# Deeper buffers for 64-bit weight units, uncopied probabilities for the second batch, and loads moved to mid-head

## The chip, the cores and the metric

One NeuronCore of a Trainium2 chip runs the whole kernel as one launch. The metric is the device time of a run in microseconds. TensorE is also called PE (its weight loads PEld), VectorE DVE, ScalarE ACT, GpSimd POOL, and SyncE SP.

## What is computed

The input is q, k and v of 4 batches, 12 heads, 448 positions and 64 features, in float32, and the weights of two feed-forward blocks, in 64-bit floats. The reference, cut to what matters:

```python
def _attn_ref(q, k, v, g_q, g_k):
    q_n, k_n = rmsnorm(q, g_q), rmsnorm(k, g_k)
    scores = (1.0 / np.sqrt(64)) * np.matmul(q_n, k_n.transpose(0, 1, 3, 2))
    scores = scores - np.max(scores, axis=-1, keepdims=True)
    attn = np.exp(scores)
    attn = attn / (np.sum(attn, axis=-1, keepdims=True) + 1e-09)
    return np.matmul(attn, v).astype(np.float32)

def _moe_ref(x, w_in, w_out):            # 768 -> 2048 -> 768
    r = np.maximum(x @ w_in, 0.0)
    return (r * r @ w_out).astype(np.float32)

def _moe2_ref(x, w1, w2, w3, w_out):     # 768 -> 1024 -> 1024 -> 768
    h = (x @ w1) * (x @ w2) @ w3
    return (h @ w_out).astype(np.float32)
```

The attention output is laid out as 1792 rows of 768, goes through the first block, and then through the second.

## The kernel before

**The heads.** The 48 heads (H = 12 of each batch) run through one loop, `for h in range(NH + 1)` (line 676). Iteration h makes the scores of head h in two halves of two blocks of 112 rows each (`stage_qk`, lines 513 to 527), their exponentials (`stage_exp`, lines 529 to 560), and for the head before the transposes of the probabilities (`stage_t`, lines 562 to 580), their low halves (`stage_lo`) and the product with v (`stage_v`, lines 614 to 630). At its end `head_prep(h + 2)` scales queries and keys of a later head (lines 474 to 499); line 496 is the last reader of a head's transposed queries. Between these steps `fill(n)` puts matmuls of other work into TensorE's order.

**The filler.** In iterations 0 to 12 it is `gen_w3o` (lines 272 to 293), which multiplies the weights w3 and w_out of the second block together. In iterations 13 to 24 it is `gen_moe(0)`, the two blocks on the first batch's rows, and so on, one batch behind the heads; the last batch's blocks come behind the loop. Every float32 product is three matmuls of fp32r halves (`mm3`, lines 260 to 264: high with high, high with low, low with high).

**The weight units.** Weights come as units of 384 or 512 columns. Those of `gen_w3o` (32 units) and of batch 0 (88 units) are 64-bit in HBM. A unit is loaded into a `raw64` tile by SP (line 180), its two words are worked on by ACT (line 194) and by POOL or ACT (lines 198 and 200), joined to a float32 by DVE (line 207), stored to HBM for the later batches (line 215), and split into a high half by ACT (line 226) and a low half by POOL or DVE (line 233, by the helper line 114). Later batches load the stored float32 units (line 183). `advance(u)` (lines 240 to 254) sets the order by hand: when the low half of unit i is made, loads go up to i + LOAD64_AHEAD, words to i + 3, joins to i + 2 and high halves to i + 1. There are four `raw64` buffers, each freed by the join.

**The probabilities.** The exponentials are written as float32 to a tile of the pool `p` (3 buffers). For heads from 12 on, a DMA on SP's queue copies that tile within SBUF into a tile of type fp32r, `pw` (3 buffers, line 549), and the transposes of line 570 read the copy as fp32r. Heads 0 to 11 are transposed from `p` as float32.

**Loads of a head.** Queries come transposed by `load_head(h + 3)` (line 414, two buffers `qt`), values by `load_v(h + 1)` (line 422, two buffers `v`), and every fourth iteration a group of four heads' rows by `load_group` (lines 405 and 406). All three stand at the start of the iteration, lines 678 to 681. SP issues these DMAs, the unit loads and stores and the copies in one order, and waits in that order for the buffers.

The framework orders the instructions of each engine from the program's text and its own costs, so that single instructions may stand some steps from their place in the text.

Of the kernel before, what the change touches and what calls it, by code (L numbers as in the profile page):

```python
# [8 lines left out]
F32 = mybir.dt.float32  # L9
F32R = mybir.dt.float32r  # L10
U16 = mybir.dt.uint16
U32 = mybir.dt.uint32
# [17 lines left out]
def attention_moe_kernel(  # L30
# [16 lines left out]
    B, P, H, C, D = q_nat.shape  # L47
    S = P * C
# [26 lines left out]
    JOIN_AHEAD = 2  # L75
    WORD_AHEAD = 3
    LOAD32_AHEAD = 3
    LOAD64_AHEAD = 5

    const = ctx.enter_context(tc.tile_pool(name="const", bufs=1))  # L80
    xp = ctx.enter_context(tc.tile_pool(name="x", bufs=8))
# [7 lines left out]
    t3 = ctx.enter_context(tc.tile_pool(name="t3", bufs=3))  # L89
# [9 lines left out]
    ident = const.tile([P, P], F32, name="ident")  # L99
    ident_r = const.tile([P, P], F32R, name="ident_r")  # L100
# [3 lines left out]
    def copy_on(eng, out, in_):  # L104
        if eng == "a":
            nc.scalar.activation(out=out, in_=in_, func=AF.Copy)  # L106
        elif eng == "g":
            nc.gpsimd.tensor_scalar(out=out, in0=in_, scalar1=1.0, scalar2=1.0, op0=ALU.mult, op1=ALU.mult)
        else:
            nc.vector.tensor_copy(out=out, in_=in_)  # L110
# [60 lines left out]
    def is64(i):  # L171
        return units[i][0].dtype != F32

    def load_next():
        i = pos["load"]
        src = units[i][0]
        n = src.shape[-1]
        if is64(i):
            t = t3.tile([128, 512, 2], U32, name="raw64", tag="raw64", bufs=4)
            nc.sync.dma_start(out=t[:, :n, :], in_=src.bitcast(U32).rearrange("p (n t) -> p n t", t=2))  # L180
        else:
            t = rawp.tile([128, 512], F32, name="raw", tag="raw")
            nc.sync.dma_start(out=t[:, :n], in_=src)
        raws[i] = t
        pos["load"] += 1
# [54 lines left out]
    def advance(u):  # L240
        while pos["lo"] <= min(u + SPLIT_AHEAD, NU - 1):
            i = pos["lo"]
            for k in range(pos["load"], min(i + LOAD64_AHEAD, NU - 1) + 1):
                if is64(k):
# [145 lines left out]
    def load_group(g):  # L390
        if not (0 <= g < NH // GH):
            return
        b, h0 = divmod(g * GH, H)
        qn = t1.tile([P, GH, C, D], F32, name="qn", tag="qn")
        kn = t2.tile([P, GH, C, D], F32, name="kn", tag="kn")
        if g == 0:
            nc.sync.dma_start(out=kn[:, 0:1], in_=k_nat[0, :, 0:1])
            load_head(0)
            nc.sync.dma_start(out=qn[:, 0:1], in_=q_nat[0, :, 0:1])
            load_to(0)  # L400
            nc.sync.dma_start(out=kn[:, 1:], in_=k_nat[0, :, 1:GH])
            nc.sync.dma_start(out=qn[:, 1:], in_=q_nat[0, :, 1:GH])
            load_to(1)
        else:
            nc.sync.dma_start(out=kn, in_=k_nat[b, :, h0:h0 + GH])
            nc.sync.dma_start(out=qn, in_=q_nat[b, :, h0:h0 + GH])
        grp[g] = [qn, kn, None, None]

    def load_head(h):
        if not (0 <= h < NH):  # L410
            return
        b, hh = divmod(h, H)
        t = t2.tile([128, S], F32, name="qt", tag="qt")
        nc.sync.dma_start(out=t, in_=q_t[b, hh])
        qts[h] = t

    def load_v(h):
        if not (0 <= h < NH):
            return
        b, hh = divmod(h, H)  # L420
        t = t2.tile([128, C, D], F32, name="v", tag="v")
        nc.sync.dma_start(out=t, in_=v_in[b, hh])
        vs[h] = t
# [77 lines left out]
    def stage_k(h):  # L501
        if not (0 <= h < NH):
            return
        d = heads[h]
        khl = d.pop("khl")
        ps = ps_kv.tile([128, 512], F32R, name="kv", tag="kv")
        for c in range(C):
            nc.tensor.transpose(ps[:, c * P:(c + 1) * P], khl[:, c, :], ident_r)  # L508
        kt = t2.tile([128, S], F32R, name="kt", tag="kt")
        copy_on("a", kt, ps[:, :S].bitcast(F32))  # L510
        d["kt"] = kt
# [17 lines left out]
    def stage_exp(h, s):  # L529
        if not (0 <= h < NH):  # L530
            return
        d = heads[h]
        nb, o = d.pop("nb"), d.pop("sc")
        i = h % 2
        if s == 0 and i == 0:
            sums2[h // 2] = small.tile([P, 2, C], F32, name="sm", tag="sm")
        sm = sums2[h // 2]
        c0 = 2 * s
        pp = t3.tile([P, 2, S], F32, name="p", tag="p")
        for j in range(2):  # L540
            c = c0 + j
            p = d["p"][c] = pp[:, j, :]
            nc.scalar.activation(  # L543
                out=p, in_=o[j], func=AF.Exp, scale=d["rq"][:, c:c + 1], bias=nb[:, j:j + 1],
                accum_out=sm[:, i, c:c + 1],
            )
        if h >= H:
            words = t3.tile([P, 2, S], F32R, name="pw", tag="pw")
            nc.sync.dma_start(out=words.bitcast(F32), in_=pp)
            d["p"][c0:c0 + 2] = [words[:, 0, :], words[:, 1, :]]  # L550
        if s == 1 and i == 1:
            nc.vector.tensor_scalar(out=sm, in0=sm, scalar1=1e-9, scalar2=None, op0=ALU.add)
            rs = small.tile([P, 2, C], F32, name="rs", tag="rs")
            nc.vector.reciprocal(out=rs, in_=sm)
            wide = t1.tile([P, C, 2, D], F32, name="rsw", tag="rsw")
            nc.gpsimd.tensor_scalar(
                out=wide, in0=rs.rearrange("p i c -> p c i").unsqueeze(3).to_broadcast([P, C, 2, D]),
                scalar1=1.0, scalar2=1.0, op0=ALU.mult, op1=ALU.mult,
            )
            sums2[h // 2] = wide.rearrange("p c i d -> p c (i d)")  # L560

    def stage_t(h, kc):
        if not (0 <= h < NH):
            return
        d = heads[h]
        k0, kn = KCS[kc]
        ps = ps_pt.tile([128, 512], F32, name="pt", tag="pt")
        to, one = (ps.bitcast(F32R), ident_r) if h >= H else (ps, ident)
        for c in range(C):
            nc.tensor.transpose(to[:kn, c * P:(c + 1) * P], d["p"][c][:, k0:k0 + kn], one)  # L570
        if kn == 128:
            t = t3.tile([128, 2, S], F32R, name="ptr", tag="ptr", bufs=3)
            hi, lo = t[:, 0, :], t[:, 1, :]
            d["pt"][kc] = [hi, lo]
        else:
            t = t1.tile([128, S], F32R, name="pte", tag="pte")
            hi, lo = t[:kn, :], t[kn:, :]
            d["pt"][kc] = [t]
        copy_on("a", hi, ps[:kn, :S])
        d["lo"].append((lo, ps[:kn, :S], hi.bitcast(F32)))  # L580

    def stage_lo(h):
        if not (0 <= h < NH):
            return
        d = heads[h]
        for lo, p, hi in d["lo"]:
            sub_on("v", lo, p, hi)
        d["lo"] = []
# [43 lines left out]
    def stage_x(h):  # L632
        if 0 <= h < NH and h % 2:
            x = xf[0]
            b, hh = divmod(h, H)
            nc.vector.tensor_tensor(out=x, in0=norms_to_rows(h), in1=x, op=ALU.mult)
            t = xp.tile([128, 2, S], F32R, name="x", tag="x")
            copy_on("a", t[:, 0, :], x)
            sub_on("g", t[:, 1, :], x, t[:, 0, :].bitcast(F32))
            xs[b, hh // 2] = t  # L640
# [7 lines left out]
    def fill(n):  # L648
        state["credit"] += n
        while state["gen"] is not None and state["credit"] > 0:  # L650
            try:
                k = next(state["gen"])
                state["credit"] -= k
                state["left"] -= k
            except StopIteration:
                state["gen"] = None
# [18 lines left out]
    first.close()  # L675
    for h in range(NH + 1):
        n = W3O / ((H + 1) * 6) if h <= H else MOE / (H * 6)
        load_head(h + 3)
        load_v(h + 1)
        if h % GH == 0:  # L680
            load_group(h // GH + 1)
        stage_qk(h, 0)
        fill(n)
        stage_exp(h, 0)
        if h % H != 1:
            stage_x(h - 2)
        stage_t(h - 1, 0)
        stage_t(h - 1, 1)
        fill(n)
        stage_lo(h - 1)  # L690
        if h < NH:
            v_prep(h)
        fill(n)
        stage_k(h + 1)
        stage_t(h - 1, 2)
        stage_t(h - 1, 3)
        fill(n)
        stage_lo(h - 1)
        stage_qk(h, 1)
        fill(n)  # L700
        stage_exp(h, 1)
        fill(n)
        stage_v(h - 1)
        if h % GH == 1:
            group_prep(h // GH + 1)
        head_prep(h + 2)
        if h and h % H == 0:
            fill(1e9)
            stage_x(h - 1)
            start_fill(gen_moe(h // H - 1), MOE)  # L710
# [57 lines left out]
```

## Time and profile before

| | |
|---|---|
| time of three runs | 1237.89, 1239.81, 1242.05 us (median 1239.81) |
| profiled execution | 1239.56 us, its span 1237.8 us |
| PE, PEld busy | 1166.3 us (94%), 1054.4 us (85%) |
| DVE, ACT, POOL busy | 710.7 us (57%), 727.7 us (59%), 784.9 us (63%) |
| mean granted TensorE clock | 0.986 |
| DMA | 207.63 MB, mean 168 GB/s |

The span is the time from the first to the last instruction. A matmul's end is modelled and matmuls overlap, so that PE can be busy all the time and yet not at its best pace; the granted clock is the share of the higher of TensorE's two levels, 1.2 and 2.4 GHz. A row of waits says which engine and line stood idle, for what, how long in all, how many times, and the longest. Waits of SP are those of its instruction order. A row of the timeline gives start, length, engine, line, operation, output<-input, the shape, the number of instructions merged, and in brackets the idle time before the first with what ended it.

### The profile page before, as it was taken

The numbers are of one execution on the slowest core, as the hardware profiler recorded it, in microseconds if no ns is written. First come the engines' busy times: TensorE is split into PE (matmuls) and PEld (weight loads), VectorE is DVE, ScalarE is ACT, GpSimd is POOL, SyncE is SP. The second block draws the span as 40 slices with busy tenths as digits, with TensorE's granted clock in tenths as the row PEclk, the third lists the DMA queues.
The fourth block names the chain that finished last, engine by engine and source line by source line (L and its number), as shares of the span: only waits on it lengthen the run. The fifth ranks groups of instructions, "written<-read, shape, count | busy, mean of one in ns | idle before, by whom it ended". The sixth has DMA issues, their size and how long they took to land.

```text
span 1237.8 us, 18914 instructions
## 1 busy us (share of the span) xinstructions
PE 1166.3 (94%) x6192; PEld 1054.4 (85%) x6192; DVE 710.7 (57%) x1314; ACT 727.7 (59%) x1553; POOL 784.9 (63%) x772
## 2 busy tenths in 40 slices
PE   3799999898898999999999999999999999999998
PEld 1588887787787888998998998999999999999998
DVE  6699888878888685546567555655664421012110
ACT  5888867667746655655645655656545554443342
POOL 5875434565776756765776664756766556678673
PEclk9899999999999999999999999999999999999999
DMA  6774547787888866455445455454444443433342
GB/s 214 242 227 131 159 140 218 254 272 249 280 259 257 257 192 194 132 155 147 148 127 154 140 155 161 143 154 121 141 138 120 135 136 112 113 109 105 105 120 93
DMA packets 111347, 207.63 MB, mean 168 GB/s; under 512 B 12208, under 2 KB 66704, under 8 KB 111248
## 3 DMA queue, kind: packets, MB, share of 16 engines
q1 hardware_dynamic: 107792, 200.92, 53.8%
q10 hardware_dynamic: 3456, 5.51, 1.2%
q8 instruction: 49, 0.80, 0.3%
q14 instruction: 50, 0.41, 0.1%
HBM read 149.95 MB, written 27.53 MB: 143 GB/s over the span
## 4 chain that ended last, share of the span: by engine, by line
PE 59%; DMA 4%; DVE 4%; ACT 2%; POOL 1%; issue 1%; ACTq 0%; SPq 0%; POOLq 0%; DVEq 0%
PE mm L262 17%; PE mm L264 17%; PE mm L263 17%; PE kv L622 3%; PE pt L570 2%; DMA pw<-p 2%; PE sc L525 1%; PE sc L524 1%; DMA raw<-w 1%; POOL hl L114 1%; ACT p L543 1%; DMA kn<-k_nat 1%; PE kv L508 1%; DVE nb L526 1%; DVE raw L207 0%
## 5 line engine op out<-in xcount | busy, mean ns | idle before, releaser
L114 POOL TENSOR_TENSOR hl<-raw,hl 128x384 fp32r<-128x384 f32 (+1 forms) x383 | 447.0, 1171 | 254.5 <-ACT hl L106 250.9
L106 ACT ACTIVATE hl<-raw 128x384 fp32r<-128x384 f32 (+1 forms) x416 | 233.8, 564 | 146.8 <-PE mm L264 82.0
L262 PE MATMUL mm<-x,hl 128*128 128x448 f32 (+1 forms) x832 | 311.3, 374 | 4.4 <-ACT x L106 1.8
L263 PE MATMUL mm<-x,hl 128*128 128x448 f32 (+1 forms) x832 | 307.2, 369 | 8.1 <-POOL x L114 8.1
L264 PE MATMUL mm<-x,hl 128*128 128x448 f32 (+1 forms) x832 | 306.4, 368 | 3.7 <-DVE hl L114 3.3
L262 PE MATMUL mm<-act,hl 128*128 128x448 f32 (+1 forms) x640 | 238.3, 372 | 0.0
L263 PE MATMUL mm<-act,hl 128*128 128x448 f32 (+1 forms) x640 | 235.7, 368 | 2.3 <-POOL act L114 2.3
L264 PE MATMUL mm<-act,hl 128*128 128x448 f32 (+1 forms) x640 | 235.0, 367 | 0.6 <-POOL hl L114 0.6
L543 ACT ACTIVATE p<-sc,nb,rr 112x448 f32<-112x448 f32 x192 | 137.4, 720 | 82.4 <-DVE nb L527 82.0
L263 PEld LDWEIGHTS mm<-x,hl 128*128 128x128 f32 x832 | 158.5, 190 | 21.9 <-POOL x L114 9.7
L262 PEld LDWEIGHTS mm<-x,hl 128*128 128x128 f32 x832 | 158.4, 190 | 19.6 <-ACT x L106 3.5
L264 PEld LDWEIGHTS mm<-x,hl 128*128 128x128 f32 x832 | 158.6, 191 | 18.3 <-DVE hl L114 4.0
L526 DVE TENSOR_REDUCE nb<-sc 112x1 f32<-112x448 f32 x192 | 113.2, 616 | 34.5 <-PE sc L525 33.0
L263 PEld LDWEIGHTS mm<-act,hl 128*128 128x128 f32 x640 | 122.0, 191 | 12.8 <-POOL act L114 3.6
L200 POOL TENSOR_SCALAR raw<-raw 128x384 uint32<-128x384 uint16 (+1 forms) x110 | 86.3, 785 | 73.3 <-DMA raw<-w_in 25.8
L264 PEld LDWEIGHTS mm<-act,hl 128*128 128x128 f32 x640 | 121.9, 190 | 10.9 <-POOL hl L114 1.3
L262 PEld LDWEIGHTS mm<-act,hl 128*128 128x128 f32 x640 | 122.2, 191 | 9.7 <-ACT act L106 0.2
L114 DVE TENSOR_TENSOR ptr<-pt,ptr 128x448 fp32r<-128x448 f32 x144 | 87.0, 619 | 71.7 <-ACT ptr L106 71.3
L207 DVE SCALAR_TENSOR_TENSOR raw<-raw 128x384 uint32<-128x384 uint32 (+1 forms) x120 | 86.8, 727 | 40.3 <-POOL hl L114 27.2
L114 POOL TENSOR_TENSOR act<-gf,act 128x448 fp32r<-128x448 f32 x80 | 97.8, 1223 | 9.5 <-ACT act L106 5.0
L194 ACT ACTIVATE raw<-raw 128x384 f32<-128x384 f32 (+1 forms) x120 | 70.7, 596 | 52.2 <-DMA raw<-w 19.6
L334 DVE TENSOR_TENSOR gf<-mm,r 128x448 f32<-128x448 f32 x64 | 39.8, 622 | 97.7 <-ACT r L330 97.3
(82 smaller groups left out, 1588.6 us busy)
## 6 DMA issues: line engine op xcount, KB each, us to landing
pw<-p SPq DMA_DIRECT2D x72, 392.0 KB, 4.2
raw<-f_in SPq DMA_DIRECT2D x96, 192.0 KB, 2.4
raw<-f_out SPq DMA_DIRECT2D x72, 256.0 KB, 2.7
raw<-f SPq DMA_DIRECT2D x96, 192.0 KB, 2.4
raw<-w_in SPq DMA_DIRECT2D x32, 384.0 KB, 4.4
raw<-w_out SPq DMA_DIRECT2D x24, 512.0 KB, 6.2
raw<-w SPq DMA_DIRECT2D x32, 384.0 KB, 4.9
raw<-w3o SPq DMA_DIRECT2D x48, 256.0 KB, 2.8
```

The lines of the kernel that those rows point to most:

```text
L106: nc.scalar.activation(out=out, in_=in_, func=AF.Copy)
L114: e.tensor_tensor(out=out, in0=in0, in1=in1, op=ALU.subtract)
L194: nc.scalar.activation(out=hi, in_=hi, func=AF.Prelu, scale=2.0**-112, alpha=-(2.0**32))
L200: nc.gpsimd.tensor_scalar(out=t[:, :n, 0], in0=low, scalar1=2.0**-13, scalar2=2.0**-14 - 0.5, op0=ALU.mult, op1=ALU.add)
L207: nc.vector.scalar_tensor_tensor(out=f[:, :n].bitcast(U32), in0=t[:, :n, 1], scalar=3, in1=t[:, :n, 0], op0=ALU.logical_shift_left, op1=AL ...
L262: nc.tensor.matmul(ps, w[:, 0, wk, :], x[0], start=(i == 0), stop=False)
L263: nc.tensor.matmul(ps, w[:, 0, wk, :], x[1], start=False, stop=False)
L264: nc.tensor.matmul(ps, w[:, 1, wk, :], x[0], start=False, stop=(i == last))
L334: nc.vector.tensor_tensor(out=gf, in0=ps, in1=r, op=ALU.mult)
L526: nc.vector.tensor_reduce(out=nb[:, j:j + 1], in_=o[j], axis=AX.X, op=ALU.max, negate=True)
L543: nc.scalar.activation(out=p, in_=o[j], func=AF.Exp, scale=d["rq"][:, c:c + 1], bias=nb[:, j:j + 1], accum_out=sm[:, i, c:c + 1],)
L622: nc.tensor.matmul(ps[:, :S], w, m, start=(n == 0), stop=(n == len(ops) - 1))
```

## The change

The 64-bit units get six buffers instead of four, and their loads go seven units ahead of the low half instead of five. The copy of the probabilities begins with head 24 instead of head 12; heads 12 to 23 are transposed from the float32 tile, as heads 0 to 11 are. The copies and the exponentials share one pool of five buffers. `load_head(h + 3)` and `load_v(h + 1)` move from the start of the iteration to behind the third `fill`, ahead of `stage_k`; `load_group` stays.

```diff
-    LOAD64_AHEAD = 5
+    LOAD64_AHEAD = 7
...
-            t = t3.tile([128, 512, 2], U32, name="raw64", tag="raw64", bufs=4)
+            t = t3.tile([128, 512, 2], U32, name="raw64", tag="raw64", bufs=6)
...
-        pp = t3.tile([P, 2, S], F32, name="p", tag="p")
+        pp = t3.tile([P, 2, S], F32, name="p", tag="p", bufs=5)
...
-        if h >= H:
-            words = t3.tile([P, 2, S], F32R, name="pw", tag="pw")
+        if h >= 2 * H:
+            words = t3.tile([P, 2, S], F32R, name="pw", tag="p", bufs=5)
             nc.sync.dma_start(out=words.bitcast(F32), in_=pp)
...
-        to, one = (ps.bitcast(F32R), ident_r) if h >= H else (ps, ident)
+        to, one = (ps.bitcast(F32R), ident_r) if h >= 2 * H else (ps, ident)
...
     for h in range(NH + 1):
         n = W3O / ((H + 1) * 6) if h <= H else MOE / (H * 6)
-        load_head(h + 3)
-        load_v(h + 1)
         if h % GH == 0:
             load_group(h // GH + 1)
...
             v_prep(h)
         fill(n)
+        load_head(h + 3)
+        load_v(h + 1)
         stage_k(h + 1)
```

## Rows read from the trace of the kernel before

**Rows 1.** Stages from:to, length, busy us by engine, granted clock, DMA share, GB/s

```profile
34.00:79.00 45.00, 35.07 (x159) 29.26 (x159) 35.05 (x60) 34.80 (x75) 35.25 (x34) 0.85 0.80 243
...
191.00:498.00 307.00, 279.95 (x1454) 249.34 (x1455) 237.37 (x419) 194.81 (x421) 191.56 (x198) 0.97 0.77 243
498.00:766.00 268.00, 265.64 (x1449) 242.33 (x1448) 158.80 (x285) 155.65 (x339) 177.27 (x166) 1.00 0.51 148
```

**Rows 2.** Waits of PE between 191 and 498 us

```profile
PE pt L570 <- DMA pw<-p: 11.1, 7, 2.6
PE sc L524 <- ACT p L543: 6.6, 6, 2.1
PE mm L264 <- DVE hl L114: 3.3, 2, 1.8
```

**Rows 3.** Waits of PE from 498 us to the end

```profile
PE pt L570 <- DMA pw<-p: 2.4, 3, 1.0
```

**Rows 4.** Timeline of PE, the waits ahead of two falls of the clock

```profile
320.28 0.70 PE L570 MATMUL pt<-ident_r,pw 112*128 112x112 f32 x6 [2.10 <-DMA pw<-p]
...
364.56 0.46 PE L524 MATMUL sc<-kt,qh 128*112 128x448 f32 x1 [2.13 <-ACT p L543]
```

**Rows 5.** Stretches of 5 us at those two falls, columns as in rows 1

```profile
320.00:325.00 5.00, 4.72 (x19) 4.29 (x20) 4.37 (x9) 3.47 (x8) 2.33 (x3) 0.66 0.93 316
365.00:370.00 5.00, 4.55 (x16) 3.87 (x15) 3.86 (x12) 2.46 (x6) 2.49 (x4) 0.66 0.72 194
```

**Rows 6.** The tile `pw` between 191 and 498 us, its issues and landings

```profile
L549 SPq DMA_DIRECT2D pw<-p x25: 517/517/521, 191.7 to 491.0; - x25
...
DMA to landing us min/median/max: 3.2/4.4/6.8
```

**Rows 7.** Waits of SP's queue between 191 and 498 us

```profile
SPq L180 <- DVE raw L207: 61.6, 35, 4.3
SPq L549 <- ACT ptr L106: 27.8, 8, 6.7
SPq L414 <- DVE ql L496: 25.2, 10, 7.3
```

**Rows 8.** Timeline of SP's queue, 228 to 239 us

```profile
228.51 0.67 SPq L215 DMA_DIRECT2D f_out<-raw  x1
236.59 0.33 SPq L414 DMA_DIRECT2D qt<-q_t  x1
...
238.26 0.60 SPq L180 DMA_DIRECT2D raw<-w_out  x1
```

**Rows 9.** Timeline of ACT at 244 us

```profile
244.18 0.69 ACT L194 ACTIVATE raw<-raw 128x512 f32<-128x512 f32 x1 [4.31 <-DMA raw<-w_out]
```

**Rows 10.** Groups by line, 191 to 498 us: busy us, mean ns, idle before

```profile
L194 ACT ACTIVATE raw<-raw 128x384 f32<-128x384 f32 (+1 forms) x78 | 45.7, 595 | 50.0 <-DMA raw<-w 19.6 <-DMA raw<-w_out 14.0 <-DMA raw<-w_in 11.4
```

**Rows 11.** Timeline of PE, eight fp32 transposes of an early head and the next

```profile
133.98 0.93 PE L570 MATMUL pt<-ident,p 112*128 112x112 f32 x8
134.68 0.42 PE L262 MATMUL mm<-x,hl 128*128 128x384 f32 x1
```

**Rows 12.** Timeline of PE, eight fp32r transposes of a later head and the next

```profile
251.15 0.73 PE L570 MATMUL pt<-ident_r,pw 112*128 112x112 f32 x8
251.72 0.44 PE L262 MATMUL mm<-act,hl 128*128 128x448 f32 x1
```

**Rows 13.** Timeline of SP's queue at the start

```profile
12.62 0.33 SPq L406 DMA_DIRECT2D qn<-q_nat  x1
15.75 0.35 SPq L414 DMA_DIRECT2D qt<-q_t  x1
16.15 1.37 SPq L180 DMA_DIRECT2D raw<-wo  x3
```

**Rows 14.** Waits of PE between 12 and 79 us

```profile
PE mm L263 <- POOL x L114: 6.7, 4, 2.9
```

## The prediction

> **What bounds the kernel now.** I read four views, from coarse to fine.
>
> First the busy time by stage [rows 1], cut at the places where the iterations over the heads change their filler. From 498 us on TensorE is all but full: 265.6 of 268 us at a granted clock of 1.00, for the twelve iterations 25 to 36. The twelve iterations 13 to 24 do the same matrix work (1454 matmuls against 1449) in 307 us, so this stage, and no later one, has time to give: some 39 us. Here the 64-bit weights of the first batch are converted; DVE is busy 237 us of it against 159, the DMA engines 0.77 against 0.51, and the clock is 0.97. The start is the second place: between 34 and 79 us PE is busy 35 of 45 us at a clock of 0.85.
>
> Second, what TensorE waits for in that stage [rows 2]. The largest row is the copied probabilities: the transposes wait 11.1 us in 7 waits for the copy `pw<-p` to land. Next are score matmuls waiting for the exponentials that free their PSUM (6.6) and weights whose low half is late (3.3). After 498 us the copies cost 2.4 us in 3 waits, and no other wait is listed [rows 3].
>
> Third, what those short waits do to the clock. The transposes at 320.28 us wait 2.10 us for the copy [rows 4], and the 5 us from 320 run at a granted 0.66, that is, mostly at 1.2 GHz [rows 5]. There are six such falls in the stage, all of about 0.66 over 5 us. Five come right behind a wait for `pw<-p`; the sixth, at 365 us, behind a wait of 2.13 us for an exponential [rows 4, 5]. Each loses 0.34 x 5 = 1.7 us.
>
> Fourth, why copies and loads are late: SP issues nearly all DMAs in one order, and waits in it. The stage has 25 copies, which take 3.2 to 6.8 us to land [rows 6]. SP's longest waits here are for buffers of 64-bit units (61.6), for an ACT instruction ahead of a copy (27.8, one row of several) and for the buffer of transposed queries (25.2 in 10 waits, one of 7.3) [rows 7]. One case can be followed to its end: SP is done with a store at 229.18 us, waits for the query buffer until 236.59, and the load of a `w_out` unit behind it leaves at 238.26 [rows 8]. ACT, which converts that data next, stands idle for 4.31 us until 244.18 [rows 9]. In all, ACT's first pass over the 64-bit units waits about 45 us for loads in this stage [rows 10].
>
> **The change part by part.** The sum is made against the profiled execution: 1239.56 us, its span of 1237.8 and 1.76 around it. It lies 0.25 us below the median of the runs shown (1239.81).
>
> *Probabilities of heads 12 to 23 are transposed uncopied.* Twenty-four copies go, and all stand in this stage. The waits for them go whole: the longest is 2.6 us [rows 2], less than the shortest landing time of 3.2 [rows 6], so the exponentials themselves were done before PE came. Term: -11.1 us. With them go five falls of the clock: 5 x 1.7 = -8.5 us (ends: 0 if other gaps take their place, -10.2 if all six go).
>
> The price is fp32 instead of fp32r in 192 transposes. Eight fp32 transposes of heads 0 to 11 hold PE for 0.70 us from the first start to the next instruction's [rows 11]; eight of the fp32r form for 0.57 [rows 12]. That makes 24 x 0.13 = +3.1 us (ends: 0, and +8 if they are split into short runs between other matmuls). All of it lies on PE, the bounding engine. Here a rule speaks against the change. The Trainium skill, FP8 and Floating Point Precision, section TensorE Precision Notes, says that true fp32 takes four passes through the array; by it the term would be some +41 us as an estimate. The rows show a ratio of 1.2 for transposes, so I keep 3.1.
>
> *Six buffers and seven units ahead, for the 64-bit units.* A load waits for the same join as before, but its data is used two units later. At 88 units in about 300 us that is 2 x 3.4 us more cover for a landing of a few us, so most of the 45 us in [rows 10] should go. *Loads of queries and values in mid-head* take the 7 us stalls such as that in [rows 8] off the loads behind them: the buffer is freed at the end of the iteration before, and at the new place that is half a head (some 12 us) past. The load's own user comes more than a head later, so it stays hidden. *The removed copies* also leave SP's order, with their waits for ACT. These three act on the same thing, late unit data, and go together. What of it reaches PE now is the waits for exponentials and for halves, 6.6 + 3.3, and a few smaller rows. I take -8 us (ends: 0, -12).
>
> *What is late next.* PE would now come 27.6 us earlier over the stage (11.1 + 8.5 + 8), and the same work of DVE would have to fit: 237 of some 290 us, 82%, where now it is 77% [rows 1]. ACT and DVE run in order, so some waits come back. I give back three tenths, +8 us (ends: 0, and all 27.6).
>
> *Buffers of probabilities:* heads 0 to 23 get five in place of three, which can only loosen; no listed wait was for them, so nothing. Heads 24 to 47 share five in place of three and three: taken at nothing, see the rivals.
>
> *The start.* The first weight units leave SP at 16.15 us, behind a query load that waited until 15.75; SP was free at 12.95 [rows 13]. They now leave some 3 us earlier, with two more in flight. PE waits 6.7 us there for a low half of `wo` units [rows 14], and the clock loses 0.15 x 45 = 6.8 us [rows 1]. I take -4 us (ends: 0, -10).
>
> Sum: -11.1 - 8.5 + 3.1 - 8 + 8 - 4 = -20.5, so 1239.56 - 20.5 = 1219.1, forecast **1219 us**. Stages past 498 us stay as they are.
>
> **The rivals.**
> *The stage becomes full:* the waits go and nothing comes back. 307 falls to the 268 of the next twelve iterations plus 3, and the start gives 5: 1239.6 - 36 - 5 = 1199. For it: the later stage shows that this is possible. Against: DVE would be at 88%. Chance 0.12.
> *The chain of DVE and ACT takes over:* PE's waits move from copies to exponentials and halves, and two thirds of the gain is given back: about 1232. For it: DVE's share, and in the stage POOL, ACT and DVE all wait for each other. Chance 0.14.
> *It doesn't do what it says:* loads are sooner issued but the DMA engines are the limit in this stretch, at 0.93 of their time in 320 to 325 us [rows 5], and the clock falls as before. About 1239. Against: the copies are bytes that go, and the mean is 0.77. Chance 0.08.
> *Slower, by the shared buffers:* in heads 24 to 47 an exponential may write only where words of three half-heads ago have been transposed. If that wait were felt by PE in each of the 24 heads with 1.0 us, the longest that is there now [rows 3], and brought a fall of 1.7 us in one of five, it would cost 24 x 1.34 = 32 us: 1251. It decides from 0.85 us a head, which cancels the gain. Against: those transposes stand ahead, in PE's order, of the scores that the exponential reads. Chance 0.09.
> *Four passes:* if fp32 transposes came to four times 0.57 us a run, the term would be 24 x 1.71 = 41 instead of 3: 1257. Heads 0 to 11 speak against it [rows 11]. Chance 0.02.
>
> **How the numbers follow.** My forecast has 0.55. Faster by over 0.3% (3.7 us, about what a measurement of this kernel can tell from no change) are the forecast, the full stage and the chain: 0.81. Within it is the fourth case, 0.08; slower are the two last, 0.11. The range of 1202 to 1240 takes in the chain and the case of no effect, and the lower ends of the start and of the late loads. It leaves out the slower cases and the deepest part of the full stage.
>
> **What would show it.** Right: iteration 25 starts some 16 to 20 us sooner, no wait of a transpose for `pw<-p` before it, one or two falls of the clock there in place of six, ACT's waits for 64-bit loads down to less than half, no SP wait of 7 us for the query buffer, fp32 transposes in runs of some 0.70 us, and the stages behind it as long as now. Wrong: as many falls of the clock behind other waits; DVE over 85% busy with PE waiting for exponentials; or waits of the exponentials after 498 us for the shared buffers.

## The result and the profile after

The changed kernel is slower: 1254.09 us against 1240.93 for the kernel before (medians of four runs each on one chip), a ratio of 1.0108 [1.0084, 1.0131]. One of the four runs of the changed kernel, 1607.88 us at a mean granted clock of 0.663 throughout, is in the median and not in the ratio; the other three take 1251.65 to 1255.34 us. The forecast was 1219, with a range of 1202 to 1240. The profile read below is that of the first experiment, the same kernel run again: span 1253.4 us, mean granted clock 0.989.

The stages of the changed kernel, cut where the filler changes as in [rows 1]; columns as there, the last two lines being single falls of the clock:

```profile
34.00:79.00 45.00, 38.63 (x177) 32.40 (x178) 34.73 (x63) 37.16 (x79) 33.99 (x32) 0.96 0.74 242
193.00:514.00 321.00, 286.00 (x1450) 250.14 (x1451) 233.64 (x416) 193.61 (x419) 186.45 (x196) 0.96 0.67 200
514.00:782.50 268.50, 266.29 (x1458) 243.27 (x1456) 160.34 (x286) 156.06 (x340) 177.33 (x166) 1.00 0.51 149
265.00:270.00 5.00, 2.20 (x5) 1.45 (x6) 1.88 (x4) 4.58 (x10) 1.81 (x2) 0.56 0.73 238
374.00:379.00 5.00, 4.20 (x13) 3.22 (x14) 4.39 (x12) 3.60 (x9) 3.19 (x4) 0.66 0.72 196
```

Nearly all of the loss, 14 of the 15.6 us between the two profiled spans, is in iterations 13 to 24: 321 us for 1450 matmuls, where 307 stood in [rows 1]; the twelve behind take 268.5 against 268. The bytes of the copies did go (DMA share 0.67 against 0.77), DVE is not busier, and the clock of the stage is still 0.96, with six falls as before (at 225, 265, 320, 375, 390 and 430 us). What TensorE waits for in this stage of the changed kernel (total, times, longest):

```profile
PE sc L524 <- ACT p L543: 20.9, 15, 4.6
PE pt L570 <- DVE ptr L114: 6.8, 8, 2.2
PE mm L264 <- POOL hl L114: 4.5, 5, 1.8
PE mm L263 <- POOL x L114: 2.0, 1, 2.0
```

The 11.1 us for the copy [rows 2] are gone, as forecast. In their place score matmuls wait 20.9 us for exponentials, not 6.6. All PE waits listed come to 35.7 us against 27.6, and PE is busy 6 us longer, of which the low clock explains some 2 us: the share that was not granted, summed over the stage, comes to 11.9 us against 10.2.

One reason why the exponentials are late shows in ACT's groups of that stage (busy us, mean ns, idle before and what ended it):

```profile
L194 ACT ACTIVATE raw<-raw 128x384 f32<-128x384 f32 (+1 forms) x75 | 44.9, 600 | 68.2 <-DMA raw<-w 29.1 <-DMA raw<-w_out 12.9 <-DMA raw<-w_in 11.7
...
L543 ACT ACTIVATE p<-sc,nb,rr 112x448 f32<-112x448 f32 x50 | 35.7, 718 | 24.8 <-DVE nb L527 24.8
...
L450 ACT ACTIVATE qn<-kn 112x1024 f32<-112x1024 f32 x3 | 3.2, 1057 | 10.5 <-DMA kn<-k_nat 10.5
```

ACT's first pass over the 64-bit units waits 29.1 + 12.9 + 11.7 = 53.7 us for loads, against 45 in [rows 10], although the program places the loads two units earlier and has two buffers more. One case can be followed in the changed kernel. SP issues a load of keys at 366.56, DVE has the exponentials' bias ready at 371.34, ACT stands in its order before two other instructions, and PE's scores come 4.62 us late. The timeline, one fence for each engine (SP, DVE, ACT, PE):

```profile
366.56 0.33 SPq L405 DMA_DIRECT2D kn<-k_nat  x1
```

```profile
370.12 1.22 DVE L527 TENSOR_TENSOR nb<-nb,rr 112x2 f32<-112x2 f32 x1
```

```profile
368.80 0.56 ACT L194 ACTIVATE raw<-raw 128x384 f32<-128x384 f32 x1 [4.10 <-DMA raw<-w]
...
372.76 1.06 ACT L450 ACTIVATE qn<-kn 112x1024 f32<-112x1024 f32 x1 [2.89 <-DMA kn<-k_nat]
373.73 0.71 ACT L543 ACTIVATE p<-sc,nb,rr 112x448 f32<-112x448 f32 x1
```

```profile
374.58 0.53 PE L524 MATMUL sc<-kt,qh 128*112 128x448 f32 x1 [4.62 <-ACT p L543]
```

The exponential could have gone at about 371.3. It went at 373.73, behind the squares of keys (line 450), which waited for a load issued only 6 us earlier: 2.4 of the 4.62 us. The granted 0.66 at 374 to 379 follows at once. The pass of line 194 did not hold this exponential: its data was there at 368.80, before the bias. Of the 20.9 us that the scores wait for exponentials, counted wait by wait, 6.0 us pass with the bias ready and ACT not yet there (5.2 of them behind line 450, here and in the wait that ends at 267.23 us, 0.5 behind a first pass); 4.4 us pass before DVE has the bias, and 10.5 us are the exponentials themselves. In the kernel before the same three parts of its 6.6 us are 0.1, 2.3 and 4.1.

DVE's order has its own late step. Its join of a unit (line 207) waits for the low half of an earlier unit on POOL, which frees the float32 buffer, and the bias of the exponentials and the low half of `ptr` can stand behind such a join. Waits of DVE at the join in the stage, in order the kernel before, the changed kernel, and the changed kernel with the hold 1 of the next section (e12):

```profile
DVE raw L207 <- POOL hl L114: 25.5, 19, 2.5
...
DVE raw L207 <- POOL hl L114: 43.2, 29, 3.5
...
DVE raw L207 <- POOL hl L114: 4.3, 4, 1.5
```

On SP the query buffer's stalls are gone and its order waits for the joins instead (before: 61.6 and 25.2 us, [rows 7]); waits of SP in the stage, changed kernel:

```profile
SPq L180 <- DVE raw L207: 147.5, 66, 5.4
...
SPq L414 <- DVE ql L496: 6.2, 5, 1.7
```

The start, changed kernel: the first weight units leave SP at 13.58 us instead of 16.15 [rows 13], but PE waits as long as in [rows 14]:

```profile
13.58 0.43 SPq L180 DMA_DIRECT2D raw<-wo  x1
```

```profile
PE mm L263 <- POOL x L114: 7.2, 4, 3.2
```

### The profile page after: what moved, and what is told of

Read it like the earlier page. It is cut to its first block, busy times and chain, and to the rows that moved or that the text cites. A ratio compares the mean times of both kernels' runs of the same rounds, so it can differ in the third digit from the quotient of the medians.

```text
span 1606.1 us, 18824 instructions
## 1 busy us (share of the span) xinstructions
PE 1575.4 (98%) x6192; PEld 1170.7 (73%) x6192; DVE 676.0 (42%) x1314; ACT 748.8 (47%) x1553; POOL 772.0 (48%) x772
## 4 chain that ended last, share of the span: by engine, by line
PE 96%; POOL 2%; issue 1%; DVE 1%; DMA 0%; SPq 0%; ACT 0%; DVEq 0%; POOLq 0%
PE mm L264 26%; PE mm L263 26%; PE mm L262 26%; PE kv L622 6%; PE pt L570 5%; PE sc L524 3%; PE sc L525 3%; PE kv L508 1%; PE mm L611 1%; POOL act L114 0%; DMA kn<-k_nat 0%; POOL x L114 0%; POOL raw L200 0%; POOL kx L480 0%; POOL khl L114 0%
## 5 line engine op out<-in xcount | busy, mean ns | idle before, releaser
L114 POOL TENSOR_TENSOR hl<-raw,hl 128x384 fp32r<-128x384 f32 (+1 forms) x383 | 435.5, 1138 | 597.5 <-ACT hl L106 595.5
L263 PE MATMUL mm<-x,hl 128*128 128x448 f32 (+1 forms) x832 | 386.7, 465 | 7.3 <-POOL x L114 7.1
L262 PE MATMUL mm<-x,hl 128*128 128x448 f32 (+1 forms) x832 | 389.0, 468 | 0.0
L264 PE MATMUL mm<-x,hl 128*128 128x448 f32 (+1 forms) x832 | 385.9, 464 | 0.0
L263 PE MATMUL mm<-act,hl 128*128 128x448 f32 (+1 forms) x640 | 297.5, 465 | 4.4 <-POOL act L114 3.2
L262 PE MATMUL mm<-act,hl 128*128 128x448 f32 (+1 forms) x640 | 298.5, 466 | 0.0
L264 PE MATMUL mm<-act,hl 128*128 128x448 f32 (+1 forms) x640 | 297.5, 465 | 0.0
L263 PEld LDWEIGHTS mm<-x,hl 128*128 128x128 f32 x832 | 173.6, 209 | 68.7 <-POOL x L114 9.4
L264 PEld LDWEIGHTS mm<-x,hl 128*128 128x128 f32 x832 | 173.7, 209 | 60.2
L262 PEld LDWEIGHTS mm<-x,hl 128*128 128x128 f32 x832 | 172.1, 207 | 60.5 <-ACT x L106 0.9
L263 PEld LDWEIGHTS mm<-act,hl 128*128 128x128 f32 x640 | 133.7, 209 | 53.0 <-POOL act L114 5.8
L264 PEld LDWEIGHTS mm<-act,hl 128*128 128x128 f32 x640 | 133.8, 209 | 46.0
L262 PEld LDWEIGHTS mm<-act,hl 128*128 128x128 f32 x640 | 133.4, 208 | 45.2 <-issue 0.3
L207 DVE SCALAR_TENSOR_TENSOR raw<-raw 128x384 uint32<-128x384 uint32 (+1 forms) x120 | 81.9, 686 | 69.6 <-POOL hl L114 57.1
L114 POOL TENSOR_TENSOR act<-gf,act 128x448 fp32r<-128x448 f32 x80 | 94.1, 1176 | 12.6 <-ACT act L333 6.6
L524 PE MATMUL sc<-kt,qh 128*112 128x448 f32 x192 | 92.3, 481 | 3.9 <-ACT p L543 2.1
```

The source lines that it names most:

```text
L114: e.tensor_tensor(out=out, in0=in0, in1=in1, op=ALU.subtract)
L207: nc.vector.scalar_tensor_tensor(out=f[:, :n].bitcast(U32), in0=t[:, :n, 1], scalar=3, in1=t[:, :n, 0], op0=ALU.logical_shift_left, op1=AL ...
L262: nc.tensor.matmul(ps, w[:, 0, wk, :], x[0], start=(i == 0), stop=False)
L263: nc.tensor.matmul(ps, w[:, 0, wk, :], x[1], start=False, stop=False)
L264: nc.tensor.matmul(ps, w[:, 1, wk, :], x[0], start=False, stop=(i == last))
L524: nc.tensor.matmul(o[j], d["qh"][:, c * P:(c + 1) * P], d["kt"], start=True, stop=False)
```

## The experiments

Ratios are to the kernel before, run on the same chip, with the 95% interval. **The lead** is counted in the traces: when ACT makes its first pass (line 194) over unit i of batch 0, the last high half it has made is that of unit i minus the lead; the mean over the 88 units. In the kernels with six buffers the program places a unit's load two units earlier, so "lead less 2" is taken to compare there.

| | median us | ratio | lead (less 2 with six buffers) |
|---|---|---|---|
| e1 the changed kernel | 1252.38 | 1.0113 [1.0093, 1.0133] | 8.0 (6.0) |
| e2 only uncopied | 1251.46 | 1.0102 [1.0084, 1.0119] | 6.0 |
| e3 only loads moved | 1242.42 | 1.0019 [1.0001, 1.0037] | 5.2 |
| e4 all but the moved loads | 1249.52 | 1.0098 [1.0073, 1.0124] | 8.0 (6.0) |
| e5 copies made, read as float32 | 1249.94 | 1.0084 [1.0063, 1.0106] | 5.5 |
| e6 copies made, not read | 1251.44 | 1.0098 [1.0077, 1.0119] | 5.5 |
| e7 all but the uncopied heads | 1239.99 | 1.0011 [0.9991, 1.0031] | 7.2 (5.2) |
| e8 six buffers, pool of five | 1239.10 | 0.9992 [0.9976, 1.0007] | 7.1 (5.1) |
| e9 uncopied, written as fp32r | 1244.58 | 1.0046 [1.0029, 1.0063] | 5.9 |

The kernel before has a lead of 5.15.

**Which part.** The changed kernel again, then one part alone or one part undone. Deeper buffers without the shared pool were not tried. The edit of e2, which is also the part that e7 undoes:

```diff
-        if h >= H:
+        if h >= 2 * H:
...
-        to, one = (ps.bitcast(F32R), ident_r) if h >= H else (ps, ident)
+        to, one = (ps.bitcast(F32R), ident_r) if h >= 2 * H else (ps, ident)
```

e3 moves the two calls and no more; e4 leaves them where they were; e8 has `LOAD64_AHEAD = 7`, `bufs=6` and the shared pool, and copies and loads as before.

> The changed kernel unaltered, for a profile at the full clock. Its time should again be about 1253 us, 12 us over the kernel before. If the loss lies in the stage of the first batch's weights (iterations 13 to 24, 307 us before), that stage is longer than 307 us; if it lies in the start, iteration 13 begins later than 191 us; if it is spread, iterations 25 to 48 are longer than 22 us each.

> Only the copies of heads 12 to 23 are taken away. If my forecast's largest terms hold (waits for the copies and falls of the clock go), 12 to 20 us faster than before. If the float32 transposes cost more than I took, or their waits come back as others, no faster, up to 10 us slower.

> Only the loads of queries and values are moved to mid-head. By my forecast 2 to 6 us faster. If the place of these loads is what makes the changed kernel slow (late in SP's order, behind unit loads that wait), 5 to 13 us slower, with waits for DMA of queries or values.

> The changed kernel with the loads left at the start of the iteration. If the move is the cause of the loss, it is faster than before by 5 to 15 us. If the deeper buffers are the cause, it stays 8 to 15 us slower than before.

> The changed kernel with heads 12 to 23 copied again (deeper 64-bit buffers, shared pool of five, moved loads). If uncopying makes the loss, it comes to the time of before or below it, 1228 to 1242 us. If the deeper buffers or the shared pool cost by themselves, it stays at 1248 or more.

> Only the deeper 64-bit buffers with the pool of five that makes room for them; copies from head 12, loads at the start of the iteration. By my forecast of late loads 4 to 12 us faster than before. If unit loads do not set the pace, within 4 us of it.

The uncopied heads alone cost as much as the whole change (1.0102 and 1.0113), and without them the rest is worth nothing (e7 1.0011, e8 0.9992). So the loss lies in the one edit that takes 24 DMAs and their waits out and reads 192 transposes as float32.

**What of that edit.** Copies can stay and be read as another type (e5), stay unread (e6), or go while the transposes keep fp32r (e9, where the exponentials of heads 12 to 23 are rounded when written, so their low bits are left out):

```diff
# e5
-            d["p"][c0:c0 + 2] = [words[:, 0, :], words[:, 1, :]]
+            d["p"][c0:c0 + 2] = [w.bitcast(F32) if h < 2 * H else w for w in (words[:, 0, :], words[:, 1, :])]
...
-        to, one = (ps.bitcast(F32R), ident_r) if h >= H else (ps, ident)
+        to, one = (ps.bitcast(F32R), ident_r) if h >= 2 * H else (ps, ident)
# e6: the same last edit, and the copies of heads 12 to 23 are not put into d["p"]
# e9
-        pp = t3.tile([P, 2, S], F32, name="p", tag="p")
+        pp = t3.tile([P, 2, S], F32R if H <= h < 2 * H else F32, name="p", tag="p")
```

> The copies of heads 12 to 23 stay, with their waits, but the transposes read the copy as float32. This is the price of float32 transposes alone, with nearly the order of before. If that price makes the loss of the uncopied kernel (12.7 us), it is 10 us or more slower than before; by my term, 3 us slower (0 to 8).

> The copies of heads 12 to 23 are still made, but nobody reads them; the transposes read the exponentials as float32. If the copies' DMA traffic or their places in SP's order mattered, it differs from the uncopied kernel (1251.5 us) by over 4 us. If the loss comes from transposes that no longer wait, so that the vector and scalar chain is ordered and pressed otherwise, it is as slow, 1248 to 1255 us, with the same waits for exponentials.

> Heads 12 to 23 uncopied, but the exponentials are written as fp32r, so that the transposes stay fp32r. It leaves out the low bits of these probabilities. If float32 transposes make the loss, it is as fast as before or faster (1225 to 1240 us). If it is the missing copies that make it (the wait moves on), it stays at 1247 to 1253 us.

With every DMA and buffer of the kernel before, and only the type of 192 transposes changed, e5 loses 10.4 us (0.84%); e9, with no fp32 transpose, loses 5.7 (0.46%). So each half of the edit is enough for a part of the loss, and neither is needed for it. A price of 10 us on PE is also not to be seen: eight such transposes take 0.70 us in the changed kernel too.

```profile
347.94 0.93 PE L570 MATMUL pt<-ident,p 112*128 112x112 f32 x8
348.64 0.45 PE L262 MATMUL mm<-act,hl 128*128 128x448 f32 x1
```

What these kernels share stands in the last column of the table: they are slower where the lead, less 2 with six buffers, is 5.5 to 6.0, and by 0.2% at most where it is 5.1 to 5.2. DVE's wait at the join sorts them too: 24.2 to 27.1 us for POOL's low halves in the kernel before, e3, e7 and e8, and 32.8 to 44.6 in the six that lose. ACT's wait for loads at the first pass does not: some 45 us in e8, in e6 and in the kernel before, 57 in e9. Each of these edits changes the order that the framework plans for ACT. These are correlations; the next runs make a test of the order.

**The order held.** Two holds keep an ACT instruction behind a named one in ACT's order, and add no wait on another engine; the framework then plans the other engines' orders with it. Hold 1: the first pass over unit i of batch 0 comes only behind the high half of unit i - 3. Hold 2: the squares of a group come only behind the last exponential in the text.

```diff
# hold 1, in the functions of lines 194 and 226
-        nc.scalar.activation(out=hi, in_=hi, func=AF.Prelu, scale=2.0**-112, alpha=-(2.0**32))
+        with tc.issue_after(his[i - 3]) if i >= U0 else ExitStack():
+            nc.scalar.activation(out=hi, in_=hi, func=AF.Prelu, scale=2.0**-112, alpha=-(2.0**32))
...
-        copy_on("a", t[:, 0, :n], raws[i][:, :n])
+        his[i] = nc.scalar.activation(out=t[:, 0, :n], in_=raws[i][:, :n], func=AF.Copy).ins
# hold 2, line 450; his["exp"] is set at line 543
-                nc.scalar.activation(out=sq[:, a:b], in_=x[:, a:b], func=AF.Square)
+            with tc.issue_after(his["exp"]) if g > 3 else ExitStack():
                 nc.scalar.activation(out=sq[:, a:b], in_=x[:, a:b], func=AF.Square)
```

| ratio to before | kernel before | only uncopied | changed | six buffers, pool of five |
|---|---|---|---|---|
| as planned | 1 | 1.0102 (e2) | 1.0113 (e1) | 0.9992 (e8) |
| hold 1 | 0.9966 [0.9954, 0.9979] (e11) | 1.0001 [0.9985, 1.0018] (e10) | 0.9976 [0.9961, 0.9991] (e12) | |
| hold 2 | | | 1.0083 [1.0058, 1.0108] (e18) | |
| both | 0.9969 [0.9952, 0.9986] (e13) | 0.9912 [0.9881, 0.9942] (e14) | 0.9895 [0.9865, 0.9924] (e15) | 0.9895 [0.9864, 0.9926] (e16) |

> The uncopied kernel, with ACT's first pass over a unit of batch 0 held behind the high half of the unit three before it, so that it is not placed earlier in ACT's order. If early passes that wait for loads, with exponentials behind them, make the loss, ACT's waits for 64-bit loads fall from 54 us to under 20 and the time falls to 1242 us or less. If the order is not the cause, it stays at 1248 to 1256 us.

> The kernel before with the same hold. If early passes cost it as well, 5 to 15 us faster than before; if they cost it little, within 4 us; slower if passes now come too late for their joins.

> The changed kernel with the same hold. Here the passes stand furthest ahead, and the six buffers bring the data early. If order is the cause of the loss, 10 us or more faster than the changed kernel (under 1243 us); if not, 1249 to 1257 us.

Hold 1 alone takes the changed kernel from 1252.38 to 1235.75 us, and the kernel before only from 1239.43 to 1234.75: of a loss of 13.7 us against the kernel before, 1.0 is left between the two held kernels, with the fp32 transposes and all else of the change in place. In the uncopied kernel the hold takes ACT's waits for 64-bit loads to 0.7 us and the time to 1239.57, and 4.8 of its 12.7 us are left against e11. ACT's groups in iterations 13 to 24 of e12 show the pass no longer waiting, and the exponentials waiting for their own input (64.0 us for DVE, where the changed kernel had 24.8), as they should if nothing stands ahead of them. The hold moves the joins as well: they stand 2.4 units ahead of the last high half in e12 and 3.6 in the changed kernel (counted as the lead is), and DVE's wait there nearly goes (4.3 against 43.2 us, above). So the runs show that the planned order makes the loss; whether ACT's passes or DVE's joins carry it to PE is not separated, as no run holds the joins alone. The load of keys is now what ACT stands for:

```profile
L194 ACT ACTIVATE raw<-raw 128x384 f32<-128x384 f32 (+1 forms) x81 | 48.2, 595 | 0.0
L543 ACT ACTIVATE p<-sc,nb,rr 112x448 f32<-112x448 f32 x50 | 35.9, 720 | 64.0 <-DVE nb L527 64.0
...
L450 ACT ACTIVATE qn<-kn 112x1024 f32<-112x1024 f32 x3 | 3.2, 1061 | 16.2 <-DMA kn<-k_nat 16.2
```

That gave hold 2, tried with hold 1 on four kernels and by itself on the changed one:

> The kernel before with two holds: ACT's first pass behind the high half of the unit three before, and the squares of a group's keys and queries (from the fifth group on) behind the last exponential of the head before them. If hoisted squares cost it too, 1228 to 1233 us; if not, 1233 to 1237 us as with the first hold alone.

> The uncopied kernel with both holds. If order makes what uncopying still costs, it comes within 3.5 us of the kernel before with both holds, about 1233 to 1236 us. If it is something else, it stays 4 to 6 us behind it, or where it was (1239 us).

> The changed kernel with both holds. If hoisted squares cost it (16 us of ACT's waits), 1228 to 1233 us; if not, 1234 to 1238 us.

> Copies from head 12 on and loads at the start, six buffers, the pool of five, and both holds. If the deeper buffers help once the order is out of the way, 2 us or more below the kernel before with both holds; if unit loads do not set the pace, the same as it within 2 us.

> The copies stay and are read as float32 for heads 12 to 23, with both holds. If the 10.4 us of the same kernel without holds were order, it is 2 to 5 us slower than the kernel before with both holds (1235.8), the float32 transposes' own time on PE. If they were a price of float32 itself, it is 8 us or more slower than that.

> The changed kernel with only the squares of the groups held. If the first pass over the units makes most of the loss, 1240 to 1250 us; if the squares make most of it, under 1236 us.

With both holds the changed kernel takes 1226.95 us (e15), faster than both kernels: 8.8 us under the kernel before with the same holds (1235.79, e13). Its stage of iterations 13 to 24, TensorE's waits there, and ACT's two groups (the squares of keys stand on line 451 in this kernel):

```profile
189.00:486.00 297.00, 279.15 (x1457) 248.79 (x1456) 246.83 (x417) 194.01 (x427) 192.76 (x196) 0.98 0.71 221
```

```profile
PE sc L524 <- ACT p L543: 6.8, 5, 2.6
PE pt L570 <- DVE ptr L114: 6.0, 5, 2.4
PE mm L264 <- POOL hl L114: 2.3, 3, 1.3
```

```profile
L194 ACT ACTIVATE raw<-raw 128x384 f32<-128x384 f32 (+1 forms) x82 | 48.6, 593 | 0.0
...
L451 ACT ACTIVATE qn<-kn 112x1024 f32<-112x1024 f32 x3 | 3.2, 1056 | 2.5 <-DVE ss L452 2.5
```

Hold 2 by itself (e18) leaves the changed kernel at 1.0083, not clear of noise below the 1.0113 without it, with ACT's first pass waiting as before for loads:

```profile
L194 ACT ACTIVATE raw<-raw 128x384 f32<-128x384 f32 (+1 forms) x76 | 45.2, 597 | 62.0 <-DMA raw<-w 25.6 <-DMA raw<-w_in 15.7 <-DMA raw<-w_out 12.1
```

So the order that goes with the pass over the units makes the loss, and the squares held back what the change could then gain, which shows only once the first is gone. In the kernel before hold 2 adds nothing to hold 1 (0.9969 and 0.9966). With both holds the buffers by themselves (e16) reach 1227.31, as much as the whole change: what the uncopied heads and the moved loads add to them can't be told from nothing. The uncopied heads without the buffers (e14, 1229.30) are 6.5 us under e13, so the two parts don't add up. That each takes out the same late data is argued, not shown. Both e14 and e15 came out below what was expected of them.

e17 is e5 with both holds: 1236.57 us, 0.9971 [0.9954, 0.9989], against 1235.79 and 0.9969 for e13, on another chip. The 10.4 us that fp32 transposes seemed to cost in e5 come to 0.8 us by the medians and 0.2 by the ratios with the order held, no more than the measurement can tell (some 3 us either way).

## Why the prediction was wrong

**What failed** is the step "What is late next". It said "ACT and DVE run in order, so some waits come back", and took three tenths, 8 us, with DVE's share in view. In the changed kernel all of the forecast gain of 27.6 us (11.1 + 8.5 + 8) came back and some 13 more (the stage is 14 us longer, of which 0.8 is for fp32). The step judged by DVE's busy share, 82% if the stage shrank; DVE is in fact busy 233.64 of 321 us, 73%. What grew is time in which DVE and ACT stand in their order for something else: 43.2 us for low halves at DVE's joins, where it was 25.5, and 53.7 us for loads at ACT's first pass, where it was 45. Under it lies an assumption that was not written down: that the instructions not named in the change keep their order. The framework plans that order, and in each kernel that loses ACT's passes over the units stand further ahead of the high halves than before. With the passes held, the loss is gone (1252.38 to 1235.75 us). In the changed kernel PE waited 14.3 us more for exponentials and 4.9 more for `ptr`.

**Copies' waits, -11.1:** right; of the 24 copies one stands ahead of the stage, at 185.40 us, but no transpose waits for `pw` before iteration 25, and in e15 none does either.

**Falls of the clock, -8.5:** wrong in the changed kernel. Six falls remain, now four behind waits for exponentials, one behind `ptr` and one behind a low half on POOL; "as many falls of the clock behind other waits" stood among the signs of being wrong, and the end "0 if other gaps take their place" came true. In e15 there are three, near 315, 360 and 430 us.

**fp32 transposes, +3.1:** not too low. A run of eight takes the 0.70 us that [rows 11] gave, and with the order held the term measures 0.8 us (e17 less e13), from which 3.1 can't be told. The Trainium skill, FP8 and Floating Point Precision, section TensorE Precision Notes, has four passes for true fp32. These transposes don't agree with it, 0.70 us against 0.57 for fp32r, and e17 excludes the estimate of +41 us.

**Late unit data, -8:** wrong in the changed kernel. The loads were placed earlier, but the pass that reads them was planned earlier by as much: lead 7.1 with six buffers alone (e8) where four give 5.15. So the data was no less late (ACT's first pass waits 45.0 us for loads in e8, as in [rows 10]), and e8 has the time of the kernel before. With both holds the same buffers give 8.5 us (1235.79 to 1227.31), close to the term.

**The start, -4:** wrong. The first weight units leave 2.6 us earlier and the clock between 34 and 79 us is 0.96, not 0.85, yet PE waits 7.2 us for the low halves. The scores of iteration 6 still begin 2.5 us earlier than before (109.0 against 111.5); by iteration 13 that is lost (193.2 against 191.0). Where it went was not followed.

**Loads in mid-head**, part of the -8 and put at 2 to 6 us by themselves in e3: SP's waits for the query buffer fell from 25.2 to 6.2 us as forecast, but the time did not (1.0019).

**The shared pool at nothing:** right. e8 has the time of the kernel before, and in the changed kernel PE waits for no exponential after 514 us, where the rival of shared buffers needed it to. Of the rivals "the chain of DVE and ACT takes over" named the right wait, with two thirds of the gain given back, and no way past zero.

What stays open: by which queue the order reaches PE, as said above; why the planner moves the passes further ahead when the transposes' type or the copies change was not looked at, only that it does. That the size of the loss in e5, e6 and e9 follows from their lead is argued from the table; those with fp32 transposes lose more than e9 at about the same lead or a lower one. Holds were tried on e5's kernel, not on e6's or e9's.

## What to carry to other kernels

Where a framework plans the order of in-order engines, an edit on one engine can reorder another: before costing it, ask which instructions stand ahead of the critical ones in each queue, and after it compare the orders, not only the waits. Here a deeper buffer did nothing while the reader was planned earlier by as much as the load; with the reader's place in its queue held, the buffers paid (nothing before, 8.5 us after). When a removed wait brings no gain, a hold on the order is a cheap test of whether the cause is the work or its order.

## What was not expected of the hardware

The low clock behind a wait of PE showed behind waits for different things and of different lengths: the wait of 4.62 us for an exponential that ended at 374.58 us was followed by 5 us at a granted 0.66, like those of 2.10 and 2.13 us in [rows 4, 5], and one of 2.21 us for `ptr` that ended at 224.92 by 5 us at 0.70. Not every wait brings it: behind one of 1.84 us that ended at 288.40 in the kernel before, the clock stayed at 1.00. And the copies within SBUF, which the change takes away, cost nothing that shows, in these two kernels, if no transpose waits for them: made and never read (e6) 1.0098, not made (e2) 1.0102.
